# A dense layer whose first block is done in two parts, with the float64 weights converted over 20 steps

## The chip, the core and the metric

The kernel runs on one NeuronCore of a Trainium2 chip. Five engines work side by side, each through its own list of instructions in order: TensorE (PE, matrix products), VectorE (DVE), ScalarE (ACT), GpSimd (POOL) and SyncE (SP, which here starts transfers). Semaphores tie them together. The metric is the time of one execution on the device in microseconds; three runs of the kernel before took 1198.01, 1201.76 and 1204.56, median 1201.76.

## The reference

Three layers in a row: attention over 4 x 448 tokens, a mixture of eight experts, and a dense layer. The change touches the dense layer alone.

```
def reference(...):
    attn_out = _attn_ref(...)                      # 4 x 12 heads x 448 x 64
    x = attn_out.transpose(0, 2, 1, 3).reshape(1792, 768)
    x = _moe_ref(x, ...)                           # 8 experts, one for each token
    return _moe2_ref(x, w_in, w_out)

def _moe2_ref(x, w_in, w_out):                     # 1792 x 768, 768 x 2048, 2048 x 768
    h = x @ w_in
    g = np.maximum(0.01 * h, h)
    return (g @ w_out).astype(np.float32)
```

`w_in` and `w_out` come as float64, and the result must be as good as one worked out in float32.

## The kernel before

**The dense stage.** The 14 tiles of 128 tokens form four blocks: 512, 512, 512 and 256 tokens. The 2048 hidden columns form 16 slices `f` of 128. A step is one block with one slice, and `run` (line 1714) takes 64 of them: block 0 with `f` = 0 to 15, then block 1 and so on. Every product is done with three matmuls, since a float32 number is split into a high part that PE takes exactly and the low rest: `h`/`l` in `yh`/`yl` (tokens, turned), `w1h`/`w1l` or `w2h`/`w2l` (weights; the names 1 and 2 alternate from step to step) and `gh`/`gl` (hidden).

**What a step issues, in this order.** `split` (line 1595) of the next step's weights: ACT copies the high part (`L1603`), and POOL or DVE subtracts it for the low one (`L1605`), once for the half of `w_in` and once for that of `w_out`. In block 0 both subtractions are POOL's, in block 1 one is POOL's and one DVE's, later both are DVE's. `l1` (line 1653): 18 matmuls into `hps`, then ACT copies them to `hs` (`L1668`), DVE makes `g` from `hps` and `hs` (`L1669`), ACT rounds it to `gh` (`L1670`), and POOL (block 0) or DVE (later) makes `gl` (`L1672`). `fetch` of the weights of three steps ahead. `l2` of the step before (line 1675): 24 matmuls into six banks `oa0` to `oa3`, `ob0`, `ob1`, which hold the sums of a block over its 16 steps. After the last, `flush` (line 1696) copies the banks to `os` (ACT 512 columns, DVE 256), and SP writes them out. In steps 9 to 14 of a block, one of six parts of the next block's tokens is turned on PE (`L1627`) and split by ACT (`yh`, `L1629`) and DVE (`yl`, `L1630`); POOL gathers those tokens (`L1614`, four indirect transfers) in step 6.

So PE's order is `l1(k)`, `l2(k-1)`, perhaps a turn, `l1(k+1)`, `l2(k)`, and what `l1(k)` gives must have passed ACT, DVE, ACT and POOL by the time `l2(k)` begins.

**The weights.** Float64 numbers are turned into float32 ones by integer work on their two words. A half (one `f`, and `a` = 0 for `w_in` or 1 for `w_out`) is loaded as 768 KB (`load64`, buffers `s`, three of them) and takes four parts (`conv_steps`, line 1542): ACT takes the magnitude `e` (`L1557`) and DVE shifts and masks (`L1558`, one input); DVE joins the sign (`L1561`); DVE joins the low word (`L1564`); DVE zeroes what is too small (`L1568`) and writes `c`. `L1561`, `L1564` and `L1568` read two inputs in SBUF. `keep` writes `c` to memory (`wc`) for the later blocks, which read it back with `load32` (line 1583). Slices 0 to 4 are converted in the expert stage. Slices 5 to 15 are converted whole by `conv` (line 1576), the two halves alternating, each in the `fetch` of one step of block 0, that is between that step's `g` and the next on DVE.

Nothing schedules the dense stage: each engine takes its instructions in the order in which `run` issues them.

Of the kernel before, what the change touches and what calls it, by code (L numbers as in the profile page):

```python
# [9 lines left out]
F32 = mybir.dt.float32  # L10
F32R = mybir.dt.float32r
# [14 lines left out]
NFLOAT = len(FLOATS)  # L26
EARLY = 5
RAW = 3
TICKS = dict(start=1189.5, const=102.3, emb=15.4, max=0.4, exp=0.16, t=15.23, hi=5.93, lo=1.08, pv=30.06, ev=0.01,
# [1462 lines left out]
class Dense:  # L1492
# [13 lines left out]
    def open(self, ctx):  # L1506
        tc = self.tc
        pool = lambda n, b, **kw: ctx.enter_context(tc.tile_pool(name=n, bufs=b, reuse_waits="tile", **kw))
        self.py = pool("d_y", 2)
        self.pg = pool("d_g", 2)  # L1510
        self.po = pool("d_o", 3)
        self.ps_h = pool("d_ps_h", 2, space=PSUM)
        self.ps_y = pool("d_ps_y", 1, space=PSUM)

    def early(self):

        if not self.wide:
            return [lambda f=f: self.load32((0, f), f) for f in range(3)]
# [22 lines left out]

    def conv_steps(self, f, a):

# [3 lines left out]
        def part(k):  # L1547
            if k == 0:
                v["s"] = self.S.pop((f, a))
                if a == 0:  # L1550
                    self.C[f] = self.pc.tile([128, 1536], F32, name="c")
                v["t"] = self.pt.tile([128, 768], I32, name="t64")
                v["e"] = self.pt.tile([128, 768], F32, name="e64")
# [40 lines left out]

    def split(self, key, a, b):
# [5 lines left out]
        c = self.C[key][:, a:a + 768]  # L1601
# [14 lines left out]

    def yt_steps(self, tiles, res):
        nc = self.nc
        T = 128 * len(tiles)
        yn = self.yn  # L1620
        res["h"] = self.py.tile([128, 6, 512], F32R, name="yh")
        res["l"] = self.py.tile([128, 6, 512], F32R, name="yl")

# [10 lines left out]
    def first_yt(self, n, res):  # L1634

        nc = self.nc
        res["h"] = self.py.tile([128, 6, 512], F32R, name="yh")
        res["l"] = self.py.tile([128, 6, 512], F32R, name="yl")
        ps = {n: self.ps_y.tile([128, 512], F32, name=n) for n in ("oa0", "oa1", "oa2", "oa3", "ob0", "ob1")}
# [13 lines left out]
    def l1(self, key, y, T, b, cut=None):  # L1653
# [13 lines left out]
        hs = self.pg.tile([128, 512], F32, name="hs")[:, 0:T]  # L1667
        nc.scalar.copy(out=hs, in_=ps[:, 0:T])  # L1668
# [5 lines left out]

    def l2(self, key, gs, o, tiles, first, last):
        nc = self.nc
        wh, wl = [t[:, 768:1536] for t in self.W[key]]
        gh, gl = gs
# [5 lines left out]
        for j in range(n):  # L1684
# [7 lines left out]
            if last and j % share == share - 1:  # L1692
                for i in range(j - share + 1, j + 1):
                    self.flush(o["a"][i], o["b"][j // share][:, 256 * (i % share):256 * (i % share) + 256], tiles[i])
# [14 lines left out]
    def head(self, part):  # L1709

        for a in (0, 768):
            self.split(part if self.wide else (0, part), a, HEAD[part][a // 768])

    def run(self):
        blocks = [list(range(0, 4)), list(range(4, 8)), list(range(8, 12)), list(range(12, 14))]
        steps = [(b, f) for b in range(4) for f in range(16)]
        key = lambda k: steps[k][1] if steps[k][0] == 0 and self.wide else steps[k]

        def fetch(k):
            if k < len(steps):  # L1720
                b, f = steps[k]
                if b == 0 and f < 3:
                    return
                if b == 0 and self.wide and f >= EARLY:
                    self.conv(f)
                else:
                    self.load32(key(k), f)

        y = {}
        self.first_yt(len(blocks[0]), y)  # L1730
        prev = None
        o = {}
        for k, (b, f) in enumerate(steps):
            T = 128 * len(blocks[b])
            if self.wide and EARLY + 1 <= k + 4 < 16:
                self.load64(k + 4, 0)
                self.load64(k + 4, 1)
            if f == 6 and b + 1 < 4:
                self.load_y(blocks[b + 1])
            if f == 7 and b + 1 < 4:  # L1740
                ny = {}
                pt = self.yt_steps(blocks[b + 1], ny)
            if k + 1 < len(steps):
                if k:
                    self.split(key(k + 1), 0, b)
                    self.split(key(k + 1), 768, b)
            g = self.l1(key(k), y, T, b, [] if k else [slice(0, 256), slice(256, 512)])
            fetch(k + 3)
            if prev:
                self.l2(*prev)  # L1750
            if 9 <= f < 15 and b + 1 < 4:
                pt[f - 9]()
            o = {} if f == 0 else o
            prev = (key(k), g, o, blocks[b], f == 0, f == 15)
            if f == 15 and b + 1 < 4:
                y = ny
        self.l2(*prev)
# [64 lines left out]
```

## Time and profile before

| | |
|---|---|
| median of three runs | 1201.76 us (1198.01 to 1204.56) |
| the profiled execution | 1202.61 us, its span 1199.6 us |
| busy in the span | PE 94%, DVE 69%, ACT 57%, POOL 48% |
| chain that ended last, by engine | PE 32%, DVE 7%, DMA 2%, issue 2% |
| mean granted clock of PE | 0.984 of full speed |

Times within the span are counted from its first instruction. The dense stage fills it from about 684 us on. A busy share is that of the whole span and mixes three layers with different limits, so a stretch is looked at by itself. The chain follows back from the last instruction to whatever released it.

### The profile page before, as it was taken

How to read it: one execution, taken by the hardware profiler on the slowest of the kernel's cores; microseconds unless marked ns; L12 is line 12 of the kernel's file. 1: busy time of each engine (PE TensorE's matmuls, PEld its weight loads, DVE VectorE, ACT ScalarE, POOL GpSimd, SP SyncE). 2: the span in 40 equal slices, each digit the busy share in tenths (PEclk: the TensorE clock that was granted, in tenths of full speed). 3: DMA queues.
4: the chain of work that ended last, by engine and by line, in shares of the span. 5: the costliest groups of instructions: out<-in, count | busy, mean ns of one | idle time of the engine just before them, and what ended most of it. 6: DMA issues, size and time to landing. Idle time of an engine off the chain costs nothing. (4 is left out here: it accounts for less than half of the span.)

```text
span 1199.6 us, 18936 instructions
## 1 busy us (share of the span) xinstructions
PE 1124.4 (94%) x6863; PEld 992.6 (83%) x6863; DVE 822.4 (69%) x1311; ACT 680.7 (57%) x1346; POOL 571.6 (48%) x488
## 2 busy tenths in 40 slices
PE   5899999999979999999899898878999999999998
PEld 3788899898868998889799786657888888888897
DVE  5899898998786778866876759897322334334464
ACT  6888898898754567556655643334433333333453
POOL 6889889691464547645745256545432120000000
PEclk9999999999989999999999999998999999999999
DMA  7789988878386888687777627755433234222552
GB/s 157 171 189 216 211 180 206 193 200 208 95 276 214 303 293 289 227 284 261 273 261 252 217 86 233 244 194 177 153 126 120 90 118 159 99 86 79 168 201 79
DMA packets 154413, 227.57 MB, mean 190 GB/s; under 512 B 60174, under 2 KB 117774, under 8 KB 154318
## 3 DMA queue, kind: packets, MB, share of 16 engines
q1 hardware_dynamic: 150990, 211.83, 58.4%
q0 software_dynamic: 2784, 12.93, 3.3%
q10 hardware_dynamic: 544, 1.57, 0.4%
q8 instruction: 55, 0.90, 0.3%
q14 instruction: 40, 0.33, 0.1%
HBM read 163.73 MB, written 30.81 MB: 162 GB/s over the span
## 5 line engine op out<-in xcount | busy, mean ns | idle before, releaser
L1669 DVE SCALAR_TENSOR_TENSOR g<-hps,hs 128x512 f32<-128x512 f32 (+1 forms) x64 | 39.8, 621 | 149.1 <-ACT hs L1668 148.9
L1016 POOL TENSOR_TENSOR w2l<-x,w2h 128x768 fp32r<-128x768 f32 x50 | 101.0, 2025 | 85.6 <-ACT w2h L1014 85.2
L1668 ACT COPY hs<-hps 128x512 f32<-128x512 f32 (+1 forms) x64 | 34.1, 532 | 159.8 <-PE hps L1663 159.8
L1016 DVE TENSOR_TENSOR w1l<-qk,w1h 128x768 fp32r<-128x768 f32 x86 | 108.6, 1275 | 15.2 <-ACT w1h L1014 15.0
L1131 PE MATMUL ya<-w2h,QB 128*128 128x512 f32 x288 | 115.4, 411 | 0.8 <-ACT QB L1229 0.8
L418 DVE TENSOR_REDUCE negm<-S 128x1 f32<-128x448 f32 x165 | 101.5, 616 | 20.9 <-PE S L414 19.6
L424 ACT ACTIVATE P<-S,negm 128x448 f32<-128x448 f32 x165 | 105.5, 640 | 11.5 <-DVE negm L418 10.4
L449 ACT CAST PH<-tp 128x512 fp32r<-128x512 f32 (+1 forms) x192 | 98.1, 532 | 15.0 <-PE tp L438 13.9
L438 PE MATMUL tp<-ident,P 128*128 128x128 f32 (+1 forms) x672 | 104.9, 277 | 1.0 <-DVE PL L452 0.9
L1111 PE MATMUL hps<-xh,w1l 128*128 128x256 f32 x336 | 95.6, 284 | 5.7 <-DVE w1l L1016 5.7
L1111 PE MATMUL hps<-xh,w1h 128*128 128x256 f32 x336 | 95.7, 285 | 1.2 <-ACT w1h L1014 1.2
L1670 ACT CAST gh<-g 128x512 fp32r<-128x512 f32 (+1 forms) x64 | 36.3, 567 | 105.9 <-DVE g L1669 105.9
L1111 PE MATMUL hps<-xl,w1h 128*128 128x256 f32 x336 | 95.1, 283 | 0.0
L438 PEld LDWEIGHTS tp<-ident,P 128*128 128x128 f32 (+1 forms) x672 | 81.6, 137 | 15.7 <-PE tp L438 1.3
L452 DVE TENSOR_TENSOR PL<-tp,PH 128x512 fp32r<-128x512 f32 (+1 forms) x144 | 86.8, 615 | 7.2 <-ACT PH L449 6.6
L1605 POOL TENSOR_TENSOR w1l<-c,w1h 128x768 fp32r<-128x768 f32 x25 | 51.9, 2091 | 66.0 <-ACT w1h L1603 66.0
L1132 PE MATMUL yb<-w2h,QB 128*128 128x256 f32 x288 | 82.2, 286 | 0.0
L1663 PE MATMUL hps<-yh,w1h 128*128 128x512 f32 (+1 forms) x198 | 73.9, 373 | 4.0 <-DVE g L1669 4.0
L1663 PE MATMUL hps<-yl,w1h 128*128 128x512 f32 (+1 forms) x198 | 72.7, 367 | 0.0
L1663 PE MATMUL hps<-yh,w1l 128*128 128x512 f32 (+1 forms) x198 | 72.5, 366 | 0.0
L1663 PE MATMUL hps<-yh,w2l 128*128 128x512 f32 (+1 forms) x192 | 69.9, 364 | 2.6 <-POOL w2l L1605 2.6
L1663 PE MATMUL hps<-yh,w2h 128*128 128x512 f32 (+1 forms) x192 | 70.7, 368 | 0.0
(324 smaller groups left out, 3671.6 us busy)
## 6 DMA issues: line engine op xcount, KB each, us to landing
c<-wc SPq DMA_DIRECT2D x50, 768.0 KB, 4.2
qk<-in_moe_w SPq DMA_DIRECT2D x44, 768.0 KB, 6.0
x<-in_moe_w SPq DMA_DIRECT2D x27, 768.0 KB, 6.6
s<-in_moe_w_in SPq DMA_DIRECT2D x16, 768.0 KB, 7.6
s<-in_moe_w_out SPq DMA_DIRECT2D x16, 768.0 KB, 4.3
wc<-c SPq DMA_DIRECT2D x16, 768.0 KB, 4.2
LL<-KL SPq DMA_DIRECT2D x46, 224.0 KB, 4.4
sq<-in_moe_w SPq DMA_DIRECT2D x13, 768.0 KB, 5.9
```

What stands on the lines that cost most here:

```text
L418: self.nc.vector.tensor_reduce(out=un["negm"][:, t:t + 1], in_=un["S", t], op=ALU.max, axis=AXX, negate=True)
L424: self.nc.scalar.activation(out=un["P"][:, t, :], in_=un["S", t], func=ACTF.Exp, bias=un["negm"][:, t:t + 1], scale=1.0, accum_out=un["den ...
L438: nc.tensor.transpose(ps[0:m, 128 * j:128 * j + 128], P[:, t, 128 * c:128 * c + m], self.ident)
L449: nc.scalar.copy(out=hi, in_=ps)
L452: nc.vector.tensor_tensor(out=lo, in0=ps, in1=hi.bitcast(F32), op=ALU.subtract)
L1016: lo.tensor_tensor(out=t[2 * m + 1][:, s, :], in0=r, in1=hi.bitcast(F32), op=ALU.subtract)
L1111: nc.tensor.matmul(ps[:, 0:T], l, r, start=(a == 0), stop=(a == len(m) - 1))
L1131: nc.tensor.matmul(y["a"][j], l, r[:, 0:512], start=st, stop=sp)
L1132: nc.tensor.matmul(y["b"][j], l, r[:, 512:768], start=st, stop=sp)
L1605: eng.tensor_tensor(out=l, in0=c, in1=h.bitcast(F32), op=ALU.subtract)
L1663: nc.tensor.matmul(ps[:, t], l, r[:, t], start=(a == 0), stop=(a == len(m) - 1))
L1669: nc.vector.scalar_tensor_tensor(out=g, in0=ps[:, 0:T], scalar=0.01, in1=hs, op0=ALU.mult, op1=ALU.max)
```

## The change

Three things change in `run`, and what they need is added elsewhere.

1. The order of the steps: block 0 with slices 0 to 7 (`PART` = 8), then block 1 with all 16, then block 0 with slices 8 to 15, then blocks 2 and 3. After the first part of block 0 its sums are copied from the banks to tiles `p` (`park`), and when the second part ends they are added to the banks on the way out (`flush`). The tokens of block 1 are gathered in step 0 and turned in steps 2 to 7; those of block 2 are gathered in step 22 and turned in 25 to 30, those of block 3 in 38 and 41 to 46. Block 0 keeps its turned tokens until step 31.
2. The conversions of slices 5 to 15 are cut into parts, which are issued six to a step, three after `fetch` and three after `l2` and the turn, from step 0 on. One half stands behind the other instead of alternating with it. A load of the half three ahead comes after a half's third part, and `keep` of a finished slice after the next `l1`. Their result `c` has two buffers of its own (`pk`). Slices 6 and 7 for block 0 and 14 and 15 for block 1 are taken from there, the others are read back from memory.
3. POOL makes both subtractions of `split` and `gl` up to step 23 (before: up to step 15 of block 0). From then on DVE does the `w_in` half and `gl`, and POOL the `w_out` half, up to the end.

`g` and `hs` have one buffer instead of two.

```
+PART = 8
-        self.py = pool("d_y", 2)
+        self.py = pool("d_y", 1)
+        self.pl = pool("d_l", 1)
+        self.pk = pool("d_k", 2)
+        self.pp = pool("d_p", 1)
...
-                    self.C[f] = self.pc.tile([128, 1536], F32, name="c")
+                    self.C[f] = (pool or self.pc).tile([128, 1536], F32, name="c")
...
-    def conv(self, f):
-        x, y = self.conv_steps(f, 0), self.conv_steps(f, 1)
-        for g, h in zip(x, y):
-            g()
-            h()
-        self.keep(f)
...
-        g = self.pg.tile([128, 512], F32, name="g")[:, 0:T]
+        g = self.pl.tile([128, 512], F32, name="g")[:, 0:T]
...
+    def park(self, a, b, t):
+
+        p = self.parked[t] = self.pp.tile([128, 768], F32, name=f"p{t}")
+        self.nc.scalar.copy(out=p[:, 0:512], in_=a)
+        self.nc.vector.tensor_copy(p[:, 512:768], b)
+
     def flush(self, a, b, t):
         nc, out = self.nc, self.out
         os = self.po.tile([128, 768], F32, name="os")
-        nc.scalar.copy(out=os[:, 0:512], in_=a)
-        nc.vector.tensor_copy(os[:, 512:768], b)
+        if t in self.parked:
+            p = self.parked.pop(t)
+            nc.vector.tensor_tensor(out=os[:, 0:512], in0=a, in1=p[:, 0:512], op=ALU.add)
+            nc.vector.tensor_tensor(out=os[:, 512:768], in0=b, in1=p[:, 512:768], op=ALU.add)
+        else:
+            nc.scalar.copy(out=os[:, 0:512], in_=a)
+            nc.vector.tensor_copy(os[:, 512:768], b)
...
-        steps = [(b, f) for b in range(4) for f in range(16)]
+        order = [(0, range(PART)), (1, range(16)), (0, range(PART, 16)), (2, range(16)), (3, range(16))]
+        steps = [(b, f, f == fs[0], f == fs[-1]) for b, fs in order for f in fs]
+
+        turns = {1: (0, range(2, PART)), 2: (PART + 14, range(PART + 17, PART + 23)), 3: (38, range(41, 47))}
+        fresh = [(f, a) for f in range(EARLY, 16) for a in range(2)] if self.wide else []
+        parts, ready, kept = [], [], []
+        for i, (f, a) in enumerate(fresh):
+            for n, c in enumerate(self.conv_steps(f, a, self.pk)):
+                parts.append(c)
+                if n == 2 and i + 3 < len(fresh):
+                    parts.append(lambda x=fresh[i + 3]: self.load64(*x))
+            if a:
+                parts.append(lambda f=f: ready.append(f))
...
-        for k, (b, f) in enumerate(steps):
+        for k, (b, f, first, last) in enumerate(steps):
             T = 128 * len(blocks[b])
-            if self.wide and EARLY + 1 <= k + 4 < 16:
-                self.load64(k + 4, 0)
-                self.load64(k + 4, 1)
...
+            late = k >= PART + 16
+            for x, (at, ks) in turns.items():
+                if k == at:
+                    self.load_y(blocks[x])
...
+            if k + 1 < len(steps) and k:
+                self.split(source(k + 1), k + 1, 0, late)
+                self.split(source(k + 1), k + 1, 768, late)
+            g = self.l1(k, y[b], T, late, [] if k else [slice(0, 256), slice(256, 512)])
+            while ready:
+                self.keep(ready.pop(0))
             fetch(k + 3)
+            convert(3)
             if prev:
                 self.l2(*prev)
...
+            convert(3)
```

The order of DVE in block 0 before, from the `g` of one step to that of the next; `t` and `s` with two numbers are the two halves of a slice:

```order
L1669 SCALAR_TENSOR_TENSOR g<-hps,hs 128x512
L1558 TENSOR_SCALAR t_9300<-s_9185 128x768
L1558 TENSOR_SCALAR t_9304<-s_9187 128x768
L1561 SCALAR_TENSOR_TENSOR t_9300<-s_9185,t_9300 128x768
L1561 SCALAR_TENSOR_TENSOR t_9304<-s_9187,t_9304 128x768
L1564 SCALAR_TENSOR_TENSOR t_9300<-s_9185,t_9300 128x768
L1564 SCALAR_TENSOR_TENSOR t_9304<-s_9187,t_9304 128x768
L1568 SCALAR_TENSOR_TENSOR c<-e_9301,t_9300 128x768
L1568 SCALAR_TENSOR_TENSOR c<-e_9305,t_9304 128x768
L1669 SCALAR_TENSOR_TENSOR g<-hps,hs 128x512
```

The order of DVE now, over two steps of those that turn tokens (`L1667` is `g`, `L1563`, `L1566`, `L1569` and `L1573` are the four parts of a conversion, `L1628` is `yl`):

```order
L1667 SCALAR_TENSOR_TENSOR g<-hps,hs 128x512
L1569 SCALAR_TENSOR_TENSOR t_9302<-s_9146,t_9302 128x768
L1573 SCALAR_TENSOR_TENSOR c<-e_9303,t_9302 128x768
L1628 TENSOR_TENSOR yl_9229<-hps,yh_9228 128x512
L1563 TENSOR_SCALAR t_9376<-s_9190 128x768
L1566 SCALAR_TENSOR_TENSOR t_9376<-s_9190,t_9376 128x768
L1667 SCALAR_TENSOR_TENSOR g<-hps,hs 128x512
L1569 SCALAR_TENSOR_TENSOR t_9376<-s_9190,t_9376 128x768
L1573 SCALAR_TENSOR_TENSOR c<-e_9377,t_9376 128x768
L1628 TENSOR_TENSOR yl_9229<-hps,yh_9228 128x512
```

Between two `g` four conversion instructions stand where eight stood, each of them reads what the one before it wrote, and `yl` stands among them.

The order of POOL at the start of the dense stage before (`gl` of step 0, then the two subtractions for step 2, `gl` of step 1, those for step 3, and `gl` of step 2):

```order
L1672 TENSOR_TENSOR gl<-g,gh 128x512
L1605 TENSOR_TENSOR w1l<-c,w1h 128x768 x2
L1672 TENSOR_TENSOR gl<-g,gh 128x512
L1605 TENSOR_TENSOR w2l<-c,w2h 128x768 x2
L1672 TENSOR_TENSOR gl<-g,gh 128x512
```

And now:

```order
L1612 DMA yn<-rows,slot 128x776 x4
L1670 TENSOR_TENSOR gl<-g,gh 128x512
L1603 TENSOR_TENSOR w1l<-c,w1h 128x768 x2
L1670 TENSOR_TENSOR gl<-g,gh 128x512
L1603 TENSOR_TENSOR w2l<-c,w2h 128x768 x2
L1670 TENSOR_TENSOR gl<-g,gh 128x512
```

The four gathers for block 1 have moved from step 6 to a place ahead of the first `gl`; the subtractions follow as before.

## Rows read from the trace of the kernel before

**Rows 1.** The page, busy tenths of the span in 40 slices.
```profile
PE   5899999999979999999899898878999999999998
DVE  5899898998786778866876759897322334334464
```
**Rows 2.** Stretches: us, busy of PE, PEld, DVE, ACT, POOL, granted clock, DMA share, GB/s.
```profile
700.52:843.65 143.13, 122.53 (x571) 99.59 (x571) 123.05 (x106) 52.85 (x77) 80.09 (x44) 0.94 0.58 193
...
833.00:836.00 3.00, 3.00 (x9) 2.38 (x9) 0.69 (x1) 2.54 (x4) 2.33 (x2) 0.57 0.99 311
...
740.00:760.00 20.00, 16.65 (x76) 13.66 (x77) 15.94 (x16) 8.00 (x12) 16.27 (x10) 0.91 0.83 272
```
**Rows 3.** The chain that ended last: start us, us, what.
```profile
700.52 4.10 PE hps L1663 x18
...
833.05 5.93 PE hps L1663 x18
...
843.65 4.13 PE hps L1663 x18
...
852.02 4.09 PE hps L1663 x18
...
860.34 4.09 PE hps L1663 x18
...
935.22 0.44 PE hps L1627 x4
```
**Rows 4.** Timeline of DVE over one step: start, us, line, instruction, count.
```profile
705.39 0.69 DVE L1669 SCALAR_TENSOR_TENSOR g<-hps,hs 128x512 f32<-128x512 f32 x1 [7.75 <-ACT hs L1668]
706.00 1.02 DVE L1558 TENSOR_SCALAR t<-s 128x768 int32<-128x768 int32 x2
...
709.78 5.11 DVE L1564 SCALAR_TENSOR_TENSOR t<-s,t 128x768 int32<-128x768 int32 x2
714.81 1.81 DVE L1568 SCALAR_TENSOR_TENSOR c<-e,t 128x768 f32<-128x768 f32 x2
716.55 0.68 DVE L1669 SCALAR_TENSOR_TENSOR g<-hps,hs 128x512 f32<-128x512 f32 x1
```
**Rows 5.** Conversion instructions on DVE, single ones, and the mask's shortest, median, longest.
```profile
709.78 2.59 DVE L1564 SCALAR_TENSOR_TENSOR t<-s,t 128x768 int32<-128x768 int32 x1
...
743.25 0.95 DVE L1564 SCALAR_TENSOR_TENSOR t<-s,t 128x768 int32<-128x768 int32 x1
...
L1558 DVE TENSOR_SCALAR t<-s x22: 542/546/1417, 706.0 to 821.6; 128x768 int32<-128x768 int32 x22
```
**Rows 6.** Timeline of DVE in the expert stage, two dependent neighbours.
```profile
427.77 1.08 DVE L1564 SCALAR_TENSOR_TENSOR t<-s,t 128x768 int32<-128x768 int32 x1
428.88 0.96 DVE L1568 SCALAR_TENSOR_TENSOR c<-e,t 128x768 f32<-128x768 f32 x1
```
**Rows 7.** Timeline of POOL: subtractions alone, `gl` and subtractions beside DVE, gathers.
```profile
695.62 3.66 POOL L1605 TENSOR_TENSOR w1l<-c,w1h 128x768 fp32r<-128x768 f32 x2
...
706.81 1.36 POOL L1672 TENSOR_TENSOR gl<-g,gh 128x512 fp32r<-128x512 f32 x1 [2.68 <-ACT gh L1670]
709.14 4.93 POOL L1605 TENSOR_TENSOR w1l<-c,w1h 128x768 fp32r<-128x768 f32 x2 [0.97 <-ACT w1h L1603]
...
741.79 1.50 POOL L1614 DMA_INDIRECT yn<-rows,slot  x1 [0.16 <-issue]
...
747.05 0.94 POOL L1614 DMA_INDIRECT yn<-rows,slot  x1 [0.30 <-issue]
```
**Rows 8.** Start of the dense stage: SP, POOL, PE, and landings of transfers that touch `rows`.
```profile
684.20 0.33 SPq L1181 DMA_DIRECT2D rows<-QA  x1
...
694.37 1.30 POOL L1672 TENSOR_TENSOR gl<-g,gh 128x512 fp32r<-128x512 f32 x1 [12.09 <-ACT gh L1670]
...
696.82 0.40 PE L1689 MATMUL oa<-w1h,gl 128*128 128x512 f32 x1
...
DMA to landing us min/median/max: 4.1/6.0/9.0
```

More of the change, by code (lines that the diff above doesn't have):

```diff
@@ L1508, in open @@
         pool = lambda n, b, **kw: ctx.enter_context(tc.tile_pool(name=n, bufs=b, reuse_waits="tile", **kw))
-        self.py = pool("d_y", 2)
+        self.py = pool("d_y", 1)
         self.pg = pool("d_g", 2)
+        self.pl = pool("d_l", 1)
         self.po = pool("d_o", 3)
+        self.pk = pool("d_k", 2)
+        self.pp = pool("d_p", 1)
+        self.parked = {}
         self.ps_h = pool("d_ps_h", 2, space=PSUM)
@@ L1517, in early @@
         if not self.wide:
-            return [lambda f=f: self.load32((0, f), f) for f in range(3)]
+            return [lambda f=f: self.load32(f, f) for f in range(3)]
         order = [(f, a) for f in list(range(EARLY - 1, 2, -1)) + [0, 1, 2, EARLY] for a in range(2)]
@@ L1540, in load64, with conv_steps @@
                               in_=self.w_in[:, cols].bitcast(I32).rearrange("(c p) f -> p c f", p=128))
-    def conv_steps(self, f, a):
+    def conv_steps(self, f, a, pool=None):
         nc = self.nc
@@ L1593, in load32, with split @@
         self.C[key] = c
-    def split(self, key, a, b):
+    def split(self, source, key, a, b):
         nc = self.nc
@@ L1600, in split @@
                            for n in (("w1h", "w1l"), ("w2h", "w2l"))[m]]
-        c = self.C[key][:, a:a + 768]
+        c = self.C[source][:, a:a + 768]
         h, l = [t[:, a:a + 768] for t in self.W[key]]
@@ L1615, in load_y, with yt_steps @@
                                          in_offset=IndirectOffsetOnAxis(ap=self.slot[:, t:t + 1], axis=0))
-    def yt_steps(self, tiles, res):
+    def yt_steps(self, tiles, res, slot):
         nc = self.nc
@@ L1620, in yt_steps @@
         yn = self.yn
-        res["h"] = self.py.tile([128, 6, 512], F32R, name="yh")
-        res["l"] = self.py.tile([128, 6, 512], F32R, name="yl")
+        res["h"] = self.py.tile([128, 6, 512], F32R, name=f"yh{slot}")
+        res["l"] = self.py.tile([128, 6, 512], F32R, name=f"yl{slot}")
         def part(c):
@@ L1636, in first_yt @@
         nc = self.nc
-        res["h"] = self.py.tile([128, 6, 512], F32R, name="yh")
-        res["l"] = self.py.tile([128, 6, 512], F32R, name="yl")
+        res["h"] = self.py.tile([128, 6, 512], F32R, name="yh0")
+        res["l"] = self.py.tile([128, 6, 512], F32R, name="yl0")
         ps = {n: self.ps_y.tile([128, 512], F32, name=n) for n in ("oa0", "oa1", "oa2", "oa3", "ob0", "ob1")}
@@ L1663, in l1 @@
                 nc.tensor.matmul(ps[:, t], l, r[:, t], start=(a == 0), stop=(a == len(m) - 1))
-        g = self.pg.tile([128, 512], F32, name="g")[:, 0:T]
+        g = self.pl.tile([128, 512], F32, name="g")[:, 0:T]
         gh = self.pg.tile([128, 512], F32R, name="gh")[:, 0:T]
         gl = self.pg.tile([128, 512], F32R, name="gl")[:, 0:T]
-        hs = self.pg.tile([128, 512], F32, name="hs")[:, 0:T]
+        hs = self.pl.tile([128, 512], F32, name="hs")[:, 0:T]
         nc.scalar.copy(out=hs, in_=ps[:, 0:T])
@@ L1673, in l1, with l2 @@
         return gh, gl
-    def l2(self, key, gs, o, tiles, first, last):
+    def l2(self, key, gs, o, tiles, first, end):
         nc = self.nc
+        last = end is not None
         wh, wl = [t[:, 768:1536] for t in self.W[key]]
@@ L1693, in l2 @@
                 for i in range(j - share + 1, j + 1):
-                    self.flush(o["a"][i], o["b"][j // share][:, 256 * (i % share):256 * (i % share) + 256], tiles[i])
+                    end(o["a"][i], o["b"][j // share][:, 256 * (i % share):256 * (i % share) + 256], tiles[i])
+    def park(self, a, b, t):
+        p = self.parked[t] = self.pp.tile([128, 768], F32, name=f"p{t}")
+        self.nc.scalar.copy(out=p[:, 0:512], in_=a)
+        self.nc.vector.tensor_copy(p[:, 512:768], b)
     def flush(self, a, b, t):
@@ L1711, in head @@
         for a in (0, 768):
-            self.split(part if self.wide else (0, part), a, HEAD[part][a // 768])
+            self.split(part, part, a, HEAD[part][a // 768])
     def run(self):
         blocks = [list(range(0, 4)), list(range(4, 8)), list(range(8, 12)), list(range(12, 14))]
-        steps = [(b, f) for b in range(4) for f in range(16)]
-        key = lambda k: steps[k][1] if steps[k][0] == 0 and self.wide else steps[k]
-        def fetch(k):
[L1720 to L1727, printed above, removed]
@@ L1729, in run @@
-        y = {}
-        self.first_yt(len(blocks[0]), y)
+        order = [(0, range(PART)), (1, range(16)), (0, range(PART, 16)), (2, range(16)), (3, range(16))]
[10 more added lines that the diff above has]
+                parts.append(lambda f=f: ready.append(f))
@@ new lines, in run, with source, convert @@
+        direct = {k for k, (b, f, *_) in enumerate(steps) if fresh and (b == 0 and EARLY < f < PART or b == 1 and f > 13)}
+        def source(k):
+            return k if k < 3 else steps[k][1] if k in direct else ("s", k)
+        def fetch(k):
+            if 3 <= k < len(steps) and k not in direct:
+                self.load32(("s", k), steps[k][1])
+        def convert(n):
+            while parts and n > 0:
+                n -= 1
+                parts.pop(0)()
+        y = {0: {}}
+        self.first_yt(len(blocks[0]), y[0])
@@ L1731, in run @@
+        if fresh:
+            self.load64(*fresh[2])
         prev = None
         o = {}
-        for k, (b, f) in enumerate(steps):
+        for k, (b, f, first, last) in enumerate(steps):
             T = 128 * len(blocks[b])
-            if self.wide and EARLY + 1 <= k + 4 < 16:
-                self.load64(k + 4, 0)
-                self.load64(k + 4, 1)
[L1738 to L1747, printed above, removed]
+            late = k >= PART + 16
+            for x, (at, ks) in turns.items():
+                if k == at:
+                    self.load_y(blocks[x])
+                if k == ks[0]:
+                    y[x] = {}
+                    pt = self.yt_steps(blocks[x], y[x], 1 if x < 3 else 0)
+            if k + 1 < len(steps) and k:
[4 more added lines that the diff above has]
+                self.keep(ready.pop(0))
@@ L1748, in run @@
             fetch(k + 3)
+            convert(3)
             if prev:
                 self.l2(*prev)
[L1751 to L1756, printed above, removed]
+            for x, (at, ks) in turns.items():
+                if k in ks:
+                    n = len(ks)
+                    for c in range(6 * ks.index(k) // n, 6 * (ks.index(k) + 1) // n):
+                        pt[c]()
@@ L1757, in run @@
+            convert(3)
+            o = {} if first else o
+            end = (self.park if b == 0 and f < PART else self.flush) if last else None
+            prev = (k, g, o, blocks[b], first, end)
         self.l2(*prev)
```

## The prediction

> **What bounds the kernel now.** I read three views: the slices, for where TensorE (PE) is not full; the chain of waits, for what ends last there; and the timeline of the engine it names. In the slices the dense stage starts near slice 24. PE falls to 7 and 8 in slices 25 to 28, where VectorE (DVE) stands at 7 to 9; after that PE is full to the end [rows 1]. The chain shows the same in steps. A step of the second block takes 860.34 - 852.02 = 8.32 us and belongs to PE alone; a step that also turns a part of the next tokens takes 0.44 more [rows 3]. In the first block the product `l1` of step 2 starts at 700.52 and that of step 15 at 843.65: 143.13 us for 13 steps, 6 of them turning. At PE's pace that is 13 x 8.32 + 6 x 0.44 = 110.8. So 32.3 us of this stretch are PE waiting, or running slowly after it had waited. DVE was busy for 123.05 of the 143.13 [rows 2], and one step shows with what: from `g` to the next `g` are 11.16 us without a gap, 0.61 for `g` and 10.55 for the eight instructions of one conversion [rows 4]. `g` stands behind the conversion on DVE, and PE needs `g` (through `gh` and `gl`).
>
> Those eight would take less by themselves. The same shift-and-or takes 0.95 us when the GpSimd queue (POOL) does arithmetic on nothing, and 2.59 when it stands beside a subtraction of the weight split [rows 5]; POOL's two subtractions take 3.66 alone and 4.93 beside DVE [rows 7]. Independent neighbours start 0.87 apart (714.81 to 716.55 is two) [rows 4]. So a conversion by itself is 2 x 0.47 (the mask's 0.55 less the same overlap of 0.08) + 6 x 0.87 = 6.16 us, and POOL's work of one step costs DVE 10.55 - 6.16 = 4.39.
>
> **What leaves.** All 11 conversions (22 halves) leave the places where one stood whole between two `g`. If nothing takes their place the gain is the 32.3. In it are 1.8 us of clock: the `l1` at 833.05 took 5.93 against 4.13 at 843.65, with 0.57 granted (part of the stretch at 1.2 GHz, the rest at 2.4) after PE had waited [rows 2, 3].
>
> **What the spread conversions cost.** There are 22 x 4 + 19 loads + 11 marks = 118 parts, six to a step: 20 steps, 1.1 halves in each. The order of DVE in front of this text shows three to five conversion instructions between two `g`. There each reads what the one before it wrote, which before was rare since two halves alternated. The one such pair in the trace has the second start 0.03 after the first ends (427.77 + 1.08 = 428.85, 428.88), where independent ones overlap by 0.08 [rows 6]. A half is then 0.58 + 0.98 + 0.98 + 0.87 = 3.41 us, and a step holds 1.1 x 3.41 = 3.75. POOL does the same two subtractions and one `gl` in each of these steps, so I add the 4.39 again, and 0.61 for `g`: 8.75 us against PE's 8.32. In the six steps that turn (2 to 7) the difference `yl` adds another 0.61: 9.36 against 8.76. DVE is over by 14 x 0.43 + 6 x 0.60 = 9.6 us. Some of that is covered: PE takes `g` through POOL, and POOL has 8.32 - 1.36 - 4.93 = 2.0 us to spare in a step [rows 7], which I count once. The term is +7.6.
> Its ends: if POOL costs each conversion only its share, DVE needs 0.55 x 10.55 + 1.22 = 7.0 and the term is 0. If every conversion instruction stands beside POOL, a half is 1.42 + 3 x 2.59 = 9.19 [rows 5], a step 10.1 + 0.61 (or + 1.22), and the term 14 x 2.4 + 6 x 2.6 - 2 = 47. I take the middle one since it comes from a step with the very same POOL work.
> The rows 6 pair is one sample, and a page says otherwise: by the Trainium skill, "VectorE: DVE Perf Modes" (section on the drain that can't be avoided), a semaphore between two neighbours costs nothing. Then a step would be 3.39 + 4.39 + 0.61 and the term 0.4. The pair speaks against it.
>
> **The start.** The four gathers of the second block's tokens now stand on POOL ahead of the first `gl`. They wait for the last rows of the expert stage, issued at 684.20; such transfers landed after 4.1 to 9.0 us [rows 8]. The gathers hold POOL 747.99 - 741.79 = 6.2 us [rows 7], `gl` takes 1.30, and PE wants it at 696.82. With the median of 6.0: 690.2 + 6.2 + 1.3 = 697.7, +0.9; ends 0 and +3.9. I take +1.0.
>
> **The clock.** Where PE waits, it may fall to the lower level as at 833. The waits forecast are under 1 us each, those of before some 2.5. Ends 0 and, with half the 10 widest waits, 5 x 1.8 = 9; I take +1.0.
>
> **What costs nothing.** (a) Parking: four ACT copies and four DVE copies stand beside the next `l1` (4.1 us), as the flush between blocks does now. When the parked sums are added, four additions at the 0.69 of `g` and four of half that size are 4.2 us of DVE, half of them before the last `l2` ends and the rest beside the next `l1`; without that cover at most 2. (b) Transfers: per step 1.65 loads or keeps and one read back, 2.65 x 0.786 = 2.1 MB in 8.32 us, 250 GB/s; 272 were moved in a stretch of before with 17% of the queues' time left [rows 2]. A load has two halves of conversion, some 15 us, to land; its wait on SP for DVE stands ahead of the read back of a step that is three steps away. If that cover went, each of some 15 steps would wait for part of a landing. (c) In blocks 2 and 3 one subtraction goes from DVE to POOL: 1.83 alone in a step of at least 4.2 (half the columns), so PE, which is the bound there, doesn't see it.
>
> **Sum.** The profiled run took 1202.61, 0.85 above the median of the runs shown. 1202.61 - 32.3 + 7.6 + 1.0 + 1.0 = 1179.9, and less 0.85: 1179.
>
> **Rivals.**
> (1) DVE keeps up: the dependent neighbours cost nothing, or POOL's ops fall into DVE's pauses. For it: DVE's own work is 3.75 of 8.32. Against it: POOL's subtractions come in each step. 1202.61 - 32.3 + 1.0 - 0.85 = 1170.5.
> (2) POOL and DVE shut each other out for whole instructions, so that each step costs DVE all of POOL's own 3.66 + 1.30 = 4.96 instead of 4.39. A step is then 3.75 + 4.96 + 0.61 = 9.32 (9.93), DVE is over by 14 x 1.0 + 6 x 1.17 - 2 = 19, and the time 1202.61 - 32.3 + 19 + 1 + 1 - 0.85 = 1190.5. For it: 2.59 is about one subtraction plus one shift-and-or. Against it: in rows 4 the loss was smaller, with both engines busy. The Trainium skill, "SBUF — State Buffer" (section on who interferes with whom), has this rule: a DVE instruction with two inputs in SBUF and a POOL instruction that reads SBUF block each other fully. The trace agrees in kind (0.95 to 2.59); by that page the time would be this rival's.
> (3) Slower than before: the conversions, now in 20 steps instead of 11, meet POOL's subtractions with every instruction. Place: DVE between two `g` of steps 0 to 19. Price: the 47 above, 1202.61 - 32.3 + 47 + 2 - 0.85 = 1218.5. It decides from the point where POOL costs DVE about 5.5 us a step instead of 4.39: 14 x (5.5 - 3.96) + 6 x (5.5 - 3.79) - 2 = 30, with the 2 of start and clock the 32. Against it: POOL has only 4.96 us of work in a step.
>
> **Chances and range.** Forecast (1173 to 1186) 0.60, rival 1 0.17, rival 2 0.17, rival 3 0.03, no change by something I have not seen 0.03. About 0.5% (6 us) is what a measurement of this kernel can tell from no change. All of the first three are faster by more: faster 0.94, same 0.03, slower 0.03. The range goes from just under rival 1 to rival 2: 1169 to 1191.
>
> **What would show it.** Right: `l1` starts 8.3 to 9.5 us apart through steps 2 to 19 and 8.32 from then on; the chain goes through DVE in part of steps 4 to 19 and through PE elsewhere; DVE over 90% busy up to step 19; conversion instructions of 0.95 and 2.59 mixed; no wait of PE at the parking or at the return to block 0. Rival 1: PE full from step 2. Rival 2: steps of 9.3 to 10. Rival 3: steps over 10.4 in twice as many places. Wrong altogether: a PE wait after step 20, a wait for `c<-wc`, or the clock low in many steps.

## The result, and the profile after

The changed kernel takes 1170.08 us (median of 4 executions, 1169.77 to 1178.41) against 1202.15 us before: a ratio of 0.9758, 95% interval 0.973 to 0.9786. It is faster, inside the range, and 9 us below the likeliest forecast: it came out as rival 1 (1170.5).

The slices of the page after, with the clock that was granted, answer to [rows 1].

```profile
PE   5899999999978999899999989999999999999998
DVE  5889898999777777877887769999942334233443
PEclk9999999999989999999999999999999999999999
```

TensorE (PE) is now full from slice 25 on (but for the last slice, as before), where it had 7 and 8. VectorE (DVE) stands at 9 in slices 25 to 29: its work was not removed, it now lies over more steps. The stretches (columns as in [rows 2]) say the same in time.

```profile
700.52:820.00 119.48, 118.29 (x605) 100.04 (x605) 117.79 (x88) 55.17 (x83) 85.53 (x42) 1.00 0.66 234
684.00:860.00 176.00, 174.81 (x907) 148.98 (x906) 169.39 (x125) 79.94 (x119) 124.22 (x64) 0.99 0.62 222
```

Both engines are busy nearly all the time, at a granted clock of 1.00. Before, PE was busy for 122.53 of 143.13 us at 0.94 [rows 2]. The chain that ended last passes through `g` for the last time at 717.87 and is PE's own after that (start, us, what; answers to [rows 3]).

```profile
717.87 0.69 DVE g L1667
718.60 4.38 PE hps L1661 x18
...
762.53 4.09 PE hps L1661 x18
770.85 4.09 PE hps L1661 x18
```

The last two products stand 8.32 us apart, as in the second block of before. One step of DVE, from `g` to `g`, answers to [rows 4, 5].

```profile
775.72 0.69 DVE L1667 SCALAR_TENSOR_TENSOR g<-hps,hs 128x512 f32<-128x512 f32 x1
776.33 1.53 DVE L1563 TENSOR_SCALAR t<-s 128x768 int32<-128x768 int32 x1
777.89 1.94 DVE L1566 SCALAR_TENSOR_TENSOR t<-s,t 128x768 int32<-128x768 int32 x1
779.86 2.49 DVE L1569 SCALAR_TENSOR_TENSOR t<-s,t 128x768 int32<-128x768 int32 x1
782.45 2.42 DVE L1573 SCALAR_TENSOR_TENSOR c<-e,t 128x768 f32<-128x768 f32 x1
784.79 0.68 DVE L1667 SCALAR_TENSOR_TENSOR g<-hps,hs 128x512 f32<-128x512 f32 x1
...
785.97 0.96 DVE L1566 SCALAR_TENSOR_TENSOR t<-s,t 128x768 int32<-128x768 int32 x1
786.96 1.95 DVE L1569 SCALAR_TENSOR_TENSOR t<-s,t 128x768 int32<-128x768 int32 x1
```

Four conversion instructions instead of eight stand between two `g`. They are still lengthened: 1.94 at 777.89, where the same instruction takes 0.96 at 785.97. From the first `l1` to the end PE waits once, for `g`, 1.1 us (waiter, what for: us in total, times, longest).

```profile
PE hps L1661 <- DVE g L1667: 1.1, 1, 1.1
```

For comparing runs I use the **dense stretch**, the time from the start of the first `g` to the end of the span, because executions of one kernel differ ahead of it. The changed kernel run again had a span of 1171.8 instead of 1168.0, but its dense stretch is the same within 0.1 us. The stages ahead took longer there: the first gather of the first block's rows starts at 676.75 instead of 673.82 us, and in both executions the transposes that open the dense stage wait some 4 us for these gathers.

All kernels of this study, spans and first `g` from their traces (us):

| kernel | median time | span | first `g` | dense stretch |
|---|---|---|---|---|
| before | 1202.15 | 1199.6 | 692.89 | 506.7 |
| after | 1170.08 | 1168.0 | 691.96 | 476.0 |
| after_again | 1172.19 | 1171.8 | 695.87 | 475.9 |
| spread_only | 1202.24 | 1200.3 | 694.12 | 506.2 |
| spread_early | 1201.02 | 1198.5 | 693.79 | 504.7 |
| bunched | 1189.41 | 1185.6 | 692.83 | 492.8 |
| fast8 | 1186.40 | 1184.5 | 696.00 | 488.5 |
| alternate | 1171.41 | 1168.5 | 691.89 | 476.6 |
| late8 | 1173.53 | 1172.9 | 696.83 | 476.1 |
| alt_late8 | 1172.21 | 1173.3 | 697.93 | 475.4 |
| before_nopool | 1169.38 | 1167.2 | 692.28 | 474.9 |
| after_nopool | 1169.43 | 1166.7 | 692.58 | 474.1 |

So of the 32.84 us between the two profiled executions (1202.61 and 1169.77) 30.7 lie in the dense stretch, 0.9 ahead of it and 1.2 outside the span.

### The profile page after: what moved, and what is told of

The parts are those of the page before. It is cut to its first block, busy times and chain, and to the rows that moved or that the text cites. A ratio compares the mean times of both kernels' runs of the same rounds, so it can differ in the third digit from the quotient of the medians.

```text
span 1168.0 us, 19046 instructions
## 1 busy us (share of the span) xinstructions
PE 1113.5 (95%) x6863; PEld 987.1 (85%) x6863; DVE 823.1 (70%) x1272; ACT 681.4 (58%) x1346; POOL 665.4 (57%) x535
## 5 line engine op out<-in xcount | busy, mean ns | idle before, releaser
L1603 POOL TENSOR_TENSOR w1l<-c,w1h 128x768 fp32r<-128x768 f32 x44 | 89.2, 2037 | 112.6 <-ACT w1h L1601 112.5
L1017 POOL TENSOR_TENSOR w2l<-x,w2h 128x768 fp32r<-128x768 f32 x50 | 101.2, 2031 | 85.8 <-ACT w2h L1015 85.4
L1603 POOL TENSOR_TENSOR w2l<-c,w2h 128x768 fp32r<-128x768 f32 x42 | 88.7, 2123 | 91.1 <-ACT w2h L1601 87.0
L1667 DVE SCALAR_TENSOR_TENSOR g<-hps,hs 128x512 f32<-128x512 f32 (+1 forms) x64 | 39.8, 622 | 134.6 <-ACT hs L1666 134.5
L439 PEld LDWEIGHTS tp<-ident,P 128*128 128x128 f32 (+1 forms) x672 | 81.6, 137 | 15.7 <-PE tp L439 1.4
L469 PE MATMUL O<-PH,vs 128*128 128x448 f32 x192 | 70.9, 398 | 0.0
```

What stands on the lines that cost most here:

```text
L439: nc.tensor.transpose(ps[0:m, 128 * j:128 * j + 128], P[:, t, 128 * c:128 * c + m], self.ident)
L1017: lo.tensor_tensor(out=t[2 * m + 1][:, s, :], in0=r, in1=hi.bitcast(F32), op=ALU.subtract)
```

## The experiments

**Theory A:** GpSimd's (POOL's) subtractions lengthen DVE's conversion instructions. With a whole conversion between two `g`, DVE needs more time per step than PE; with 1.1 halves it just fits. **Rivals:** evenness alone cures it, in any order of the blocks (B); only the total counts, not the single step (C); the conversion's own work or its transfers are late, whatever POOL does (D).

**after_again**, no edit.

> The changed kernel once more, as the reference for its neighbours on the same chip. 1168 to 1175 us in every theory; the 1178.41 of one earlier run should not come back in most of these.

Measured: 1172.19 (1170.1 to 1176.15), ratio 0.9758 [0.972, 0.9796]. The result repeats; one of the four executions lies above the expected 1175.

**before_nopool: take POOL's subtractions away from the kernel before.**

```diff
-        eng.tensor_tensor(out=l, in0=c, in1=h.bitcast(F32), op=ALU.subtract)
+        if b == 7:
+            nc.scalar.copy(out=l, in_=c)
+        else:
+            eng.tensor_tensor(out=l, in0=c, in1=h.bitcast(F32), op=ALU.subtract)
...
-                    self.split(key(k + 1), 0, b)
-                    self.split(key(k + 1), 768, b)
+                    self.split(key(k + 1), 0, b or 7)
+                    self.split(key(k + 1), 768, b or 7)
```

(`b` is 0 in block 0, so every subtraction that is issued there from step 1 on becomes a copy by ScalarE)

> The kernel before, with GpSimd's two weight subtractions of the first block's steps 2 to 15 replaced by ScalarE copies of the whole slice (this leaves out the low parts of those weights). Theory A (GpSimd's subtractions hold VectorE's conversion, 10.55 us of which 6.16 are its own): a step needs 6.8 us of VectorE, TensorE is the bound, the 32 us go: 1169 to 1174 us; the shift-and-or takes 0.95 throughout. Rival D (the conversion's own work or its loads are what is late): 1190 us or more.

Measured: 1169.38, ratio 0.9734 [0.9697, 0.9771]. The stretch in which PE had been busy for 122.53 of 143.13 us [rows 2] now reads:

```profile
700.52:843.65 143.13, 143.13 (x732) 121.17 (x731) 99.29 (x122) 87.78 (x128) 30.76 (x21) 1.00 0.67 226
```

PE has no gap at all, with the conversions where they were, whole between two `g`. The shift-and-or of the conversion (`L1564`) takes 946 ns in the mean, where it took 2222 in before:

```profile
L1564 DVE SCALAR_TENSOR_TENSOR t<-s,t 128x768 int32<-128x768 int32 x22 | 20.0, 946 | 0.0
```

Rival D falls: conversions and loads do no harm by themselves. Theory A holds. That POOL's results by themselves come too late for PE is no rival for most of the gain: in the changed kernel POOL makes the same subtractions, and PE waits 1.1 us in all.

**after_nopool: the same in the changed kernel** (steps 2 to 24, `gl` stays on POOL).

> The changed kernel, with GpSimd's two weight subtractions of steps 2 to 24 replaced by ScalarE copies (this leaves out the low parts of those weights); gl stays on GpSimd. Theory A (GpSimd's subtractions hold VectorE for about 3.9 us a step, which the trace shows as longer conversion instructions): VectorE's busy time from 684 to 860 us falls from 169 to about 100 us, no conversion instruction over 1.5 us, time 1168 to 1170 us since TensorE is the bound there already. Rival F (the long instructions come from transfers or from ScalarE): busy stays over 140 us with many of 2 us or more.

Measured: 1169.43; DVE's busy time from 684 to 860 went from 169.39 to 114.88, not to 100, and 19 of the 88 conversion instructions took over 1.5 us (1.66 to 1.95), where I had expected none. I had forgotten to count `gl`. Rival F falls: no instruction took 2 us. The conversion groups of that stretch (line, instruction, count | busy us, mean ns | idle before), in before, in after, and without the subtractions:

```profile
L1564 DVE SCALAR_TENSOR_TENSOR t<-s,t 128x768 int32<-128x768 int32 x22 | 48.0, 2222 | 0.0
L1561 DVE SCALAR_TENSOR_TENSOR t<-s,t 128x768 int32<-128x768 int32 x22 | 32.7, 1523 | 0.0
L1568 DVE SCALAR_TENSOR_TENSOR c<-e,t 128x768 f32<-128x768 f32 x22 | 20.0, 946 | 0.0
L1558 DVE TENSOR_SCALAR t<-s 128x768 int32<-128x768 int32 x22 | 14.7, 695 | 5.9 <-DMA s<-in_moe_w_out 5.9
```

```profile
L1573 DVE SCALAR_TENSOR_TENSOR c<-e,t 128x768 f32<-128x768 f32 x22 | 42.9, 1951 | 0.9
L1569 DVE SCALAR_TENSOR_TENSOR t<-s,t 128x768 int32<-128x768 int32 x22 | 39.4, 1792 | 0.6
L1563 DVE TENSOR_SCALAR t<-s 128x768 int32<-128x768 int32 x22 | 36.2, 1646 | 0.0
L1566 DVE SCALAR_TENSOR_TENSOR t<-s,t 128x768 int32<-128x768 int32 x22 | 32.8, 1491 | 0.5
```

```profile
L1569 DVE SCALAR_TENSOR_TENSOR t<-s,t 128x768 int32<-128x768 int32 x22 | 30.9, 1403 | 0.6
L1573 DVE SCALAR_TENSOR_TENSOR c<-e,t 128x768 f32<-128x768 f32 x22 | 24.9, 1134 | 0.9
L1566 DVE SCALAR_TENSOR_TENSOR t<-s,t 128x768 int32<-128x768 int32 x22 | 21.0, 956 | 0.5
L1563 DVE TENSOR_SCALAR t<-s 128x768 int32<-128x768 int32 x22 | 17.7, 804 | 0.0
```

Alone, the four take 546 + 3 x 946 = 3384 ns as independent neighbours [rows 5] and 546 + 3 x 960 = 3426 as dependent ones. What the means exceed that is POOL's **hold**:
- before: (2222 + 1523 + 946 + 695 - 3384) x 22 = 44.0 us, 4.0 for each of 11 slices;
- after: (1951 + 1792 + 1646 + 1491 - 3426) x 22 = 76.0 us, 3.8 for each of 20 steps;
- without the subtractions: (1403 + 1134 + 956 + 804 - 3426) x 22 = 19.2 us, 1.0 a step, beside what POOL still does there, almost only `gl`.

So the subtractions hold DVE for 3.8 - 1.0 = 2.8 us a step. (The copies in their place load ScalarE, 110.76 us busy instead of 79.94.) PE has no wait left, and the dense stretch is 474.1; in before_nopool, in the old order, it is 474.9. Against the 506.7 of before that is 31.8 to 32.6 lower; the change got 30.7 of it.

**spread_only: the even spread without the new order of the blocks.**

```diff
-order = [(0, range(PART)), (1, range(16)), (0, range(PART, 16)), (2, range(16)), (3, range(16))]
+order = [(b, range(16)) for b in range(4)]
-turns = {1: (0, range(2, PART)), ...
+turns = {1: (6, range(9, 15)), ...
-            convert(3)   ...   convert(3)
+            convert(5)   ...   convert(4)
```

(with four instead of two buffers for the converted slices, no parked sums, and POOL's part ending with step 15 as before)

> The order of the blocks as before (0, 1, 2, 3 whole, nothing parked), the 118 parts of the conversions spread evenly, nine to a step, over steps 0 to 13. Theory A (in this stretch VectorE has more to do than TensorE: own 1.68 halves x 3.41 = 5.7 us, 3.5 to 4.4 lost to GpSimd's subtractions, 0.61 for g, 0.3 for yl in the mean, together 10.1 to 11.0 us a step against 8.5): 13 steps lose 21 to 32 us against the changed kernel, 1190 to 1202 us. Rival B (a whole conversion between two g was the whole trouble, evenness alone cures it): 1170 to 1173 us.

Measured: 1202.24, ratio 1.0006 [0.999, 1.0022]: nothing gained. This is just past the upper end of theory A, and rival B falls. One step took 15.4 us, so I removed what made it long:

**spread_early: spread_only with the gathers of the second block moved from step 6 to step 0.**

```diff
-turns = {1: (6, range(9, 15)), ...
+turns = {1: (0, range(9, 15)), ...
```

> The order of the blocks as before with the 118 parts spread nine to a step, now with the four gathers of the second block's tokens at step 0 instead of step 6, where they had put GpSimd's subtractions back to back and one conversion instruction had taken 9.35 us. Theory A (the block holds more VectorE work than TensorE work, whatever the order within it): that step falls from 15.4 to about 10.3 us, the stretch from the first g to the end from 506.2 to 499 to 502 us, the time 1193 to 1199 us. Rival B' (without that one stall the evenness would have cured the rest): 476 to 482 us for the stretch, 1171 to 1177 us. Rival I (the stall is no loss, its time is made up elsewhere): 505 to 507 us, as before.

Measured: 1201.02, ratio 0.9994 [0.9977, 1.0012]; dense stretch 504.7, not 499 to 502. The long step fell to 10.6 as expected, but the step before it, 8.0 in spread_only, rose to 11.1: the block's total hardly moved. I had priced one step alone; rival I is nearer. From the first `g` to the 14th are 137.1 us, 10.55 a step, by DVE's work: 13 x 9/118 x 22 halves x 3.41 = 74.4, `g` 13 x 0.61 = 7.9, four `yl` 2.4, and the rest, 52.4, is hold: 4.0 a step. With POOL's subtractions beside them the conversions find no room in one block, however even they are (without the subtractions, in before_nopool, even whole ones do). The new order gives them 20 steps instead of 14. The old order with the subtractions given to another engine, as late8 below does in the new one, was not tried.

**bunched: the new order, a whole slice in every second step.**

```diff
-            convert(3)   ...   convert(3)
+            convert(0 if k % 2 else 11)   ...
```

> The changed order of the blocks, but a whole slice (11 parts) between two g in every second step and nothing in the other, same total over steps 0 to 20. Theory A with the timing of g as the cause: a step with a slice has 2 x 3.41 + about 4.4 + 0.61 = 11.8 us on VectorE against 8.32; some 2 us of it are slack of the g chain, so each of 11 steps loses 0.5 to 2 us and the empty step between gives no time back to TensorE: 1176 to 1191 us, best guess 1181. Rival C (only the total per step counts, lateness is made up in the empty steps): 1169 to 1172 us.

Measured: 1189.41, ratio 0.9907 [0.9876, 0.9938]; dense stretch 492.8, 16.7 over the changed kernel. DVE is busy for less of the stretch than in the changed kernel, not more, and yet late in places:

```profile
684.00:860.00 176.00, 168.32 (x846) 142.21 (x845) 127.82 (x110) 73.84 (x110) 108.97 (x59) 0.96 0.60 210
```

The time lies in theory A's range, but its mechanism is not what the trace shows. In steps 10 to 19 the `l1` start 8.32 us apart, as in the changed kernel, though from `g` to `g` a full step takes 11.7 to 14.1 us and an empty one 3.4 to 4.9 (`l1` on PE, then `g` on DVE):

```profile
808.55 4.09 PE hps L1661 x18
816.87 4.10 PE hps L1661 x18
```

```profile
805.10 0.69 DVE L1667 SCALAR_TENSOR_TENSOR g<-hps,hs 128x512 f32<-128x512 f32 x1 [4.22 <-ACT hs L1666]
817.53 0.68 DVE L1667 SCALAR_TENSOR_TENSOR g<-hps,hs 128x512 f32<-128x512 f32 x1
821.74 0.69 DVE L1667 SCALAR_TENSOR_TENSOR g<-hps,hs 128x512 f32<-128x512 f32 x1 [3.53 <-ACT hs L1666]
```

There an empty step gives back all that the full one before it took, as rival C has it. Step by step against the changed kernel, the loss stands elsewhere: 3.5 us in steps 2 and 3, 1.0 in steps 5 and 7, 7.4 at the parking, 0.8 in step 20 and 4.1 in step 23, where POOL's subtraction stands behind the gathers of block 2. Rival C's time (1169 to 1172) falls because of these places. The largest is a cover that my prediction named and that is gone here, the parking: its copy stood behind a whole slice.

```profile
PE ob L1689 <- DVE p L1699: 4.6, 1, 4.6
```

After that wait PE also ran slower: the granted clock is 0.54 between 777 and 783 us.

**fast8: eight parts a step from step 6 on.**

```diff
-            convert(3)   ...   convert(3)
+            convert(3 if k < 6 else 4)   ...   convert(3 if k < 6 else 4)
```

> The changed kernel with eight parts instead of six in each of steps 6 to 16, so the conversions end four steps earlier. Theory A (VectorE at its edge: own work plus what GpSimd takes): a step has 1.49 x 3.41 + 3.9 + 0.61 = 9.6 us against 8.32, ten such steps less 2 us of slack cost about 11: 1178 to 1184 us. Rival B (VectorE has room, its 99% busy is only waiting that fills what is free): 1169 to 1172 us.

Measured: 1186.40, ratio 0.9862 [0.983, 0.9894]; dense stretch 488.5, 12.5 over the changed kernel where 11 were expected (the profiled execution, 1186.31, is over the expected range because its first `g` came 4 us later than in the first execution of after). Ten steps from the 7th `g` on take 101.2 us, 10.1 each. DVE is at its edge in the changed kernel: a third more conversion per step, and PE waits, mostly for `gl` and `gh`, which POOL and ScalarE make from a late `g`.

```profile
PE oa L1688 <- POOL gl L1670: 4.3, 7, 1.0
...
PE oa L1688 <- ACT gh L1668: 3.0, 3, 1.9
```

**alternate: the two halves of a slice alternate, so that neighbours do not depend on each other.**

```diff
-for i, (f, a) in enumerate(fresh):
-    for n, c in enumerate(self.conv_steps(f, a, self.pk)):
-        parts.append(c)
+    halves = [self.conv_steps(f, h, self.pk) for h in range(2)]
+    for n in range(4):
+        for h in range(2):
+            parts.append(halves[h][n])
...
```

> The changed kernel with the two halves of a slice alternating within the six parts of a step, so that neighbours do not depend on each other. Theory A with 0.11 us for each dependent neighbour: 22 halves x (3.41 - 3.08) = 7 us less of VectorE from 684 to 860 us (169 to about 162), the time 1168 to 1171 us, with less spread between executions. Rival G (dependence costs nothing): busy 168 to 171, time as the changed kernel.

Measured: 1171.41 (1168.88 to 1173.17), ratio 0.9746 [0.9722, 0.9771]; dense stretch 476.6. The conversion instructions:

```profile
L1569 DVE SCALAR_TENSOR_TENSOR t<-s,t 128x768 int32<-128x768 int32 x22 | 47.3, 2169 | 0.0
L1573 DVE SCALAR_TENSOR_TENSOR c<-e,t 128x768 f32<-128x768 f32 x22 | 38.6, 1788 | 0.0
L1566 DVE SCALAR_TENSOR_TENSOR t<-s,t 128x768 int32<-128x768 int32 x22 | 35.5, 1644 | 0.0
...
L1563 DVE TENSOR_SCALAR t<-s 128x768 int32<-128x768 int32 x22 | 14.2, 676 | 0.0
```

They are busy for 135.6 us against 151.3, 15.7 less, twice the 7 expected; rival G falls. Most of it is not the 0.11 us of each pair: the hold fell from 76.0 to (2169 + 1788 + 1644 + 676 - 3384) x 22 = 63.6 us, 3.2 a step instead of 3.8, which is 12.4 of the 15.7; why, was not tried. The time did not move, since PE is the bound. With less spread I was wrong; as far as the profiled executions show, the spread comes from ahead of the dense stretch.

**late8: VectorE does `gl` and the w_in half of the subtraction from step 8 on.**

```diff
-            late = k >= PART + 16
+            late = k >= PART
```

> The changed kernel with VectorE instead of GpSimd doing gl and the w_in half of the subtraction from step 8 on (as it does from step 24 on). Theory A (half of GpSimd's work held VectorE for as long as VectorE now needs to do it itself): a step has 3.75 + 0.61 + 0.96 + 0.69 + about 1.9 of hold = 7.9 us against 8.2 before, time 1168 to 1172 us. Rival E (GpSimd's hold does not shrink with its work): 9.5 us or more a step, 12 steps x 1.2 - 2, 1180 to 1184 us.

Measured: 1173.53 (1169.86 to 1175.42), ratio 0.9755 [0.9721, 0.9788]; dense stretch 476.1, as the changed kernel. In the 168 us from the first `g` on DVE takes over 13 subtractions and 12 `gl` and is still busy for less: 157.21 us instead of 165.58. Rival E falls: the work that POOL did beside it had cost DVE more than doing it.

**alt_late8: both together.**

> The changed kernel with alternating halves and with VectorE instead of GpSimd doing gl and the w_in half from step 8 on. Theory A: VectorE gets slack, so what TensorE still waits in the dense stage (from the first g to the end 476.0 us against 474.1 without GpSimd's subtractions) goes in part: 474.5 to 475.8 us for that stretch, 1168 to 1173 us in all, the spread coming from the stage before. Rival H (the remaining waits are not VectorE's load but gl queued behind a subtraction on GpSimd, or the uneven steps): 476.0 or more for the stretch, the time as the changed kernel.

Measured: 1172.21 (1171.58 to 1175.26), ratio 0.9753 [0.9724, 0.9781]; dense stretch 475.4. Of the 1.9 us that were left 0.6 went, within the expectation and against rival H, though by one execution; in the time that can't be told from the changed kernel. No version here beats it by a measurable amount, and by the floor of 474.1 none with these edits can.

## Why the prediction was right, and which term was not

**What bounds: right, with one reading too narrow.** The 32.3 us of TensorE's waits were the whole of it: before_nopool and after_nopool, which take the cause away, measure a floor 31.8 and 32.6 us lower. That POOL's lengthening of the conversions is the cause is shown by before_nopool, not only read. But `g` was not alone behind them. PE's waits in the stretch of 143.13 us in before (as in the result: total, times, longest):

```profile
PE hps L1627 <- DVE yl L1630: 7.4, 4, 2.6
...
PE oa L1689 <- ACT gh L1670: 5.0, 3, 2.3
...
PE hps L1663 <- DVE g L1669: 4.0, 1, 4.0
...
PE hps L1663 <- POOL w2l L1605: 2.6, 1, 2.6
```

The longest in sum is for `yl`, which stands in the same queue behind a conversion; the 2.6 are for a subtraction that stood behind the gathers of step 6. PE was idle for 143.13 - 122.53 = 20.6 of the 32.3 us. In the other 11.7 it worked, but slower: the mean granted clock of 0.94 [rows 2] is worth 0.06 x 143.13 = 8.6 us by my estimate, where I had read 1.8 from one product.

**A conversion by itself, 6.16: right.** Dependent neighbours at +0.03: right, as 785.97 + 0.96 = 786.93 and the next at 786.96. A half has 3.41 us by that. By the page "VectorE: DVE Perf Modes" of the Trainium skill (the drain that can't be avoided) a semaphore between two neighbours costs nothing, and by that these would have been free. The gap of 0.03 against the overlap of 0.08 [rows 4], and alternate, 15.7 us shorter without the dependence, go against that.

**The step that failed: the +7.6, "I add the 4.39 again" less 2.0 of slack.** Two parts of it were mis-sized.

The hold of 4.39 came from one step [rows 4]. It was a typical one: 6 of the 11 slices of before were held 4.36 to 4.38 us, four 4.0 to 4.1, and one, while POOL gathered, 1.05, which makes the mean 4.0. In the changed kernel it is 3.8 in the mean of 20 steps, with which a step of DVE is 3.75 + 3.8 + 0.61 = 8.16 against PE's 8.32, and 8.77 against 8.76 in the six that turn. But this mean hides two stretches. From the `g` of step 1 to that of step 10 are 75.06 us, 8.34 a step, while the `l1` of PE start 8.84 apart in the mean: DVE catches up. In steps 5, 7 and 9 it was held 1.65 to 2.62 only. From the `g` of step 10 (775.72) to that of step 19 (853.77) are 78.05 us, 8.67 a step, held 4.25 in the mean. There DVE was over PE's 8.32 by 0.35, nearly the 0.43 of the forecast, and PE never waited.

PE did not wait since the slack is larger than the 2.0 that I took from POOL's spare time. In a step that turns nothing PE needs its `g` only after the next `l1`. In the changed kernel `g` starts 5.03 us after the first matmul of its `l1` in step 10 and 8.21 after it in step 19, where the conversions end:

```profile
845.56 0.40 PE L1661 MATMUL hps<-yh,w2h 128*128 128x512 f32 x1
```

```profile
853.77 0.68 DVE L1667 SCALAR_TENSOR_TENSOR g<-hps,hs 128x512 f32<-128x512 f32 x1
```

In bunched a distance of 10.21 (step 17) cost PE nothing, and one of 11.07 (step 19) cost 0.8. So some 5 us are covered, not 2.0, and 2.0 of them were left when the conversions ended. The term is 0 instead of 7.6. The mechanism was right. That the excess of steps 10 to 19 ended before the slack did was not foreseen: to that extent it is luck that the time came out at the low end of the range.

**Start: 0 instead of 1.0.** The last thing that the gathers (POOL) wait for is, by the profile, the transposes. They start at 686.81, 3.6 us after the last rows were issued (683.24) and not the 6.0 that I had added for the landing; `gl` is done before PE asks (compare [rows 8]).

```profile
686.81 0.97 POOL L1612 DMA_INDIRECT yn<-rows,slot  x1 [5.49 <-PE oa L1641]
...
693.39 1.89 POOL L1670 TENSOR_TENSOR gl<-g,gh 128x512 fp32r<-128x512 f32 x1 [1.86 <-ACT gh L1668]
```

```profile
695.90 0.40 PE L1688 MATMUL oa<-w1h,gl 128*128 128x512 f32 x1
```

693.39 + 1.89 = 695.28, 0.6 ahead of 695.90. What the start did cost I had not priced: the conversions begin in step 0, so the `g` of step 1 comes 9.56 us after its `l1` began, and PE's one wait of 1.1 us stands ahead of the `l1` of step 3.

**Clock: 0 instead of 1.0.** No wait is longer than 1.1 us, and the granted clock is 1.00 between 700 and 820.

**What costs nothing: right.** No wait at the parking, at the return to block 0 or in blocks 2 and 3. The cover was real: bunched lost it at the parking, for 4.6 us.

**The sum.** 1179.9 less 7.6, 1.0 and 1.0, plus 1.6 of the ceiling that did not come (32.3 - 30.7, of which 1.1 is the one wait), less 0.9 ahead of the stretch and 1.2 outside the span, is 1169.8, the profiled execution's 1169.77.

**The rivals.** Rival 1's time is what happened, though for neither of its two reasons: the neighbours are not free, and POOL's work doesn't vanish in pauses. DVE keeps up in steps 1 to 10 and falls behind in 10 to 19, within the slack. Rival 2 (4.96 a step) is not what the means show: 3.8 to 4.0 in after, before and spread_early. The page "SBUF — State Buffer" of the Trainium skill (who interferes with whom) is right in kind, as before_nopool shows. It says that the order of issue decides which engine blocks, so that all of POOL's time falls on DVE was my reading of it. Measured are about 0.8 of POOL's own 4.96 us, and POOL is held too (4.93 instead of 3.66 [rows 7]). Rival 3's mechanism exists: the hold in all rose from 44 to 76 us because 20 steps meet POOL instead of 11. It did not decide, since 3.8 is far from its 5.5.

## What to carry to other kernels

Where two engines share a step, add up for the slower one its own work and its hold by the other, and compare with the bound over several steps, not one. Then ask how late its result may come before the bound engine waits: here some 5 us, so that in bunched even steps of 14 us, with steps of 3.4 between them, cost nothing. What did cost were the places where PE needed something else that stood behind a long piece of work, the parked sums above all. And make sure that there are enough steps: evenness in the old order gained 2.0 us of the dense stretch at most, the new order with a whole slice in every second step 13.9, both together 30.7.

## What the runs showed of the hardware

- A single DVE instruction can be held far longer than one POOL instruction. In spread_only, where the gathers had delayed POOL's work so that it stood back to back, a mask of 0.55 us took 9.35 (first DVE, then POOL):

```profile
754.22 9.35 DVE L1563 TENSOR_SCALAR t<-s 128x768 int32<-128x768 int32 x1
763.60 0.96 DVE L1566 SCALAR_TENSOR_TENSOR t<-s,t 128x768 int32<-128x768 int32 x1
```

```profile
754.72 3.61 POOL L1603 TENSOR_TENSOR w2l<-c,w2h 128x768 fp32r<-128x768 f32 x2
758.30 1.26 POOL L1670 TENSOR_TENSOR gl<-g,gh 128x512 fp32r<-128x512 f32 x1
759.53 3.62 POOL L1603 TENSOR_TENSOR w1l<-c,w1h 128x768 fp32r<-128x768 f32 x2
```

POOL ran five instructions without a gap, from 754.72 to 763.15, at the speed that it has alone ([rows 7]: 3.66 for two), and DVE's one ended 0.4 us later.
- `g` and `yl`, which read PSUM, took 0.68 to 0.69 each time in the changed kernel (at 512 columns 0.676 at least, 0.692 at most); the conversions beside the same POOL work took up to 2.63 instead of 0.96.
- Independent neighbours not only overlap, they are also held less: 3.2 us a step against 3.8. The cause stays open.
